# LSH attention with a routed MoE: the first head pair's projections, mask loads and factors in another order

## The chip, the cores and the metric

The kernel runs on one core of one Trainium2 chip. The metric is the device time of one execution in microseconds; three runs of the kernel before gave 714.1, 710.82 and 713.1, median 713.1. All times in the trace are in microseconds from the start of the profiled span.

## The reference

Attention with 4 batches, 8 heads, 768 tokens and 64 channels in which a query sees only the keys of its own hash bucket, then a mixture of 8 experts with one expert per token:

```python
q_bits = (np.einsum('bhsd,dk->bhsk', q, proj) > 0)      # 6 bits
k_bits = (np.einsum('bhsd,dk->bhsk', k, proj) > 0)
mask = q_bucket[:, :, :, None] == k_bucket[:, :, None, :]
scores = np.where(mask, scale * np.matmul(q, k.transpose(0, 1, 3, 2)), -1000000000.0)
attn = softmax(scores); out = np.matmul(attn, v)        # written out in the reference
x = out.transpose(0, 2, 1, 3).reshape(B * S, H * D)
expert_idx = argmax(x @ w_gate); y = relu(x @ w1[e]) @ w2[e]; return gate_w * y
```

## The kernel before

Two heads of one batch make a pair, and 16 pairs are worked one behind the other. A pair has 12 units: 128 queries of one head against all 768 keys. In the first pair units 0 to 2 and 3 to 5 are the two heads, in later ones the heads alternate; units 6 to 11 are the second half of the queries. Every instruction's place on its engine is written out by hand: a list of words for the first pair (`HEAD`, L956 to L960), one for each further pair (`PLAN`), one for the last (`LAST`), and `step` (L1025) turns a word into instructions. Each engine works its instructions in the order of the words.

What a word does (the digits behind it are the unit, or the head, and the part):

- S: the four matmuls of a unit's scores on TensorE, two with the low parts and the mask rows (L309), two with the high parts (L311). Three score tiles in PSUM; a fourth score waits for the exponential that read the first.
- R: the negated row maximum (`peak`, L319) on VectorE. In the first pair and the last pair R also makes the two factors that the exponential takes, scale and bias (`factor`, L324 and L326), on VectorE. In the pairs between, a word A makes them, on the engine that its letter names (P is GpSimd; there the second operation is L328).
- X: the exponential on ScalarE (L335), with the row sums.
- T and E: transposes of the exponentials on TensorE for units 0 to 5 (L349) and the copies out of PSUM, on ScalarE (E..a, L375) or VectorE (E..v, L373). D: 32x32 turns of units 6 to 11 on VectorE (L389); Y: SyncE then sends them between partitions, eight transfers a word (L400). B: products with the values (L411).
- G, H, w: the projections for the bucket bits of the next pair on TensorE (`lsh_mm`, L264; two PSUM tiles of the same two that T, B and K use), their signs on ScalarE (L244) and the store of the bits to memory (L277, L278; the store on SyncE).
- s and z: head 2 or 3 is split into parts of higher and lower precision on GpSimd (`split`, L192 to L199; head 2 is `w_214` in the order, head 3 `w_337`, their input `w_69`), and the bits are read back as mask rows of that head (`mask`, L282, issued by GpSimd). The word s04 makes the half of head 2's queries that unit 12, the first of pair 1, reads; s05 the other half. C words do the same for pairs from the third on.

On SyncE, loads of inputs and values and fills of rows in memory are issued ahead of a score by `before` (L1001), between the store of the bits and the exchange.

Of the kernel before, what the change touches and what calls it, by code (L numbers as in the profile page):

```python
# [15 lines left out]
B, H, S, D = 4, 8, 768, 64  # L16
# [3 lines left out]
NG = B * NP  # L20
# [36 lines left out]
def lsh_attention_moe(ctx, tc, qk2, v, proj, wg, w1, w1q, w2, out):  # L57
    nc = tc.nc
# [16 lines left out]
    def load_x(h):  # L75
        g = h // 2
        if g == NG - 1:
            x = (wk if h % 2 else moe).tile([128, 2 * S], F32, name="xl" if h % 2 else "xhe", bufs=1)
        else:
            x = room[:, h % 2] if g % 2 else wk.tile([128, 2 * S], F32, name="xd")  # L80
        for c in ((S, 2 * S), (0, S)) if h < 2 else ((0, 2 * S),):
            nc.sync.dma_start(x[:, c[0]:c[1]], qk2[h][:, c[0]:c[1]])
        XD[h] = x

    def load_v(g):
        VT[g] = wk.tile([128, NT, 2, D], F32, name="vt")
        nc.sync.dma_start(VT[g], v[g])
# [60 lines left out]
    def fill(e):  # L148

        nc.sync.dma_start(xs[e * ROW:e * ROW + FILL].rearrange("(p j) w -> p j w", p=128),  # L150
                          C["empty"][:, 0:1].to_broadcast([128, FILL // 128, RW]))
# [135 lines left out]
    def unit(i):  # L287

        g, r = divmod(i, 12)
        hf, r = divmod(r, 6)  # L290
        t, s = divmod(r, 2)
        if i < 6:
            s, t = divmod(r, 3)
        return g, hf, s, t

    def score(i, parts=None):
        parts = parts or ((False, True) if i < 4 else (True, False))
        g, hf, s, t = unit(i)
        k = QK[2 * g + s]
        if i not in SC:  # L300
            SC[i] = ps.tile([128, 2, 512], F32, name="s", bufs=3)
        p = SC[i]
        c = slice((3 * hf + t) * 128, (3 * hf + t) * 128 + 128)

        for low in parts:
            for a in range(2):
                n = slice(a * HALF, (a + 1) * HALF)
                if low:
                    nc.tensor.matmul(p[:, a, :HALF], k[0:80, 2, c], k[0:80, 3, n], start=i >= 4, stop=i < 4)  # L309
                else:  # L310
                    nc.tensor.matmul(p[:, a, :HALF], k[:, 0, c], k[:, 1, n], start=i < 4, stop=i >= 4)  # L311

    def peak(i):
        g, hf, s, t = unit(i)
        p = SC[i]
        if i % 6 == 0:
            SM[g, hf] = wk.tile([128, 3, 3], F32, name="sm", bufs=4)[:, :, 0:2]
        m = MB[i] = wk.tile([128, 4], F32, name="m", bufs=5)
        nc.vector.tensor_reduce(m[:, 0:1], p[:, :, :HALF], axis=AX.XY, op=OP.max, negate=True)  # L319

    def factor(i, eng):

        m = MB[i]
        eng.tensor_scalar(m[:, 1:2], m[:, 0:1], -FLOOR, D ** -0.5, op0=OP.is_lt, op1=OP.mult)  # L324
        if eng is nc.vector:
            eng.tensor_scalar(m[:, 2:3], m[:, 0:1], m[:, 1:2], None, op0=OP.mult)  # L326
        else:
            eng.tensor_tensor(m[:, 2:3], m[:, 0:1], m[:, 1:2], op=OP.mult)  # L328
# [54 lines left out]
    def turn(i):  # L383

        g, j = divmod(i, 12)
        if g not in DT:
            DT[g] = moe.tile([128, 4, 6, NT, 32], F32, name="w2")
        d = DT[g][:, :, j - 6]
        nc.vector.transpose(d.rearrange("p b k q -> p k b q"), PP.pop(i).rearrange("p a c -> p (a c)"))  # L389
# [14 lines left out]
    def pv(u, kt):  # L404
        g, hf = divmod(u, 2)
        if kt == 0:
            PV[u] = ps.tile([128, 512], F32, name="t", bufs=2)
        p = PV[u]
        for s in range(2):
            x = PT[u][:, :, s::2, kt].rearrange("p a t q -> p t a q") if turned(u) else PT[u][:, s, kt, :]  # L410
            nc.tensor.matmul(p[s * 64:(s + 1) * 64, :HALF], VT[g][:, kt, s, :], x,  # L411
                             start=(kt == 0), stop=(kt == NT - 1))

    def pv_end(u):
        OT[u] = wk.tile([128, HALF], F32, name="ot")
        nc.scalar.activation(OT[u], PV.pop(u)[:, :HALF], AF.Copy)
# [515 lines left out]
    def weight_half(op, x):  # L932
# [22 lines left out]

    HEAD = """  # L956
        k01A k00V j00V j01P y01 q00A p00V y00 q01P l00V b03 p01P f0 b00 b02 l01P b01 k10A f1 k11A y11 j10P p10A R0
        q10A S1 j11P b12 y10 R1 l10P b13 S2 X0 b10 p11P s01 R2 X1 b11 S3 q11P S4 X2 G H w R3 T00 T01 E00a l11P S5 R4
        E01a T02 X3 s00 R5 E02a s02 T10 X4 S6 E10v X5 R6 T11 S7 s10 E11a T12 s13 R7 E12a T20 X6 S8 s03 E20v T21 X7
        S9 z0 E21a T22 s11 R8 E22a D6 S10 s14 R9 X8 s15 D7 S11 R10 X9 s12 z1 B00 D8 R11 s05 X10 B01 s04 X11  # L960
    """.split()

    PLAN = """
# [37 lines left out]
    def before(c):  # L1001

        g, r = divmod(c, 6)
        if r == 3 and g + 2 < NG:
            load_x(2 * g + 4)
            load_x(2 * g + 5)
        if g + 1 < NG and r == (5 if g else 4):
            load_v(g + 1)
        for e in {(0, 1): (0,), (0, 2): (1,), (0, 3): (2,), (0, 4): (3,), (1, 4): (4,), (2, 4): (5,), (3, 4): (6,), (4, 4): (7,)}.get((g, r), ()):
            fill(e)  # L1010

    def behind(i):

        if i % 2 == 0:
            return
        c = i // 2
        if c == NC - 6:
            rows(0)
        if c >= NC - 6:
            weights((1, 1, 1, 2, 1, 2)[c - NC + 6])  # L1020
# [3 lines left out]
    def step(g, w):  # L1024

        prev = w.count("-")
        w = w.rstrip("-")
        n = g - prev
        if n < 0 or (g == NG and not prev):
            return  # L1030
        op, x = w[0], w[1:]
        if op == "S":
            i = 12 * n + int(x)
            if i % 2 == 0:
                before(i // 2)
            score(i)
        elif op == "R":
            i = 12 * n + int(x)
            peak(i)
            if not 0 < n < NG - 1:  # L1040
                factor(i, nc.vector)
                behind(i)
        elif op == "A":
            factor(12 * n + int(x[:-1]), ENG[x[-1]])
        elif op == "B":
            for kt in range(3 * int(x[1]), 3 * int(x[1]) + 3):
                pv(2 * n + int(x[0]), kt)
        elif op == "D":
            turn(12 * n + int(x))
        elif op == "Y":  # L1050
            exchange(n, ((0, 1), (2, 3))[int(x)])
        elif op == "C":
            part(2 * n + 2 + int(x[0]), int(x[1]))
        elif op == "Z":
            route_step(n, int(x))
        elif op == "N":
            scatter_step(n, int(x))
        elif op == "X":
            expo(12 * n + int(x))
        elif op == "T":  # L1060
            trans(6 * n + int(x[0]), int(x[1]))
        elif op == "E":
            trans_ev(6 * n + int(x[0]), int(x[1]), x[2] == "v" and not (n % NP == 1 and n > NP and x in FREE))
        elif op == "V":
            for kt in range(NT):
                pv(2 * n + int(x[0]), kt)
        elif op == "O":
            pv_end(2 * n + int(x))
        elif op == "M":
            sums(2 * n + int(x))  # L1070
        elif op == "K":
            TK[2 * n + int(x)] = tok(2 * n + int(x))
        elif op == "L":
            tok_ev(2 * n + int(x), TK.pop(2 * n + int(x)))
        elif op == "G" and n + 1 < NG:
            lsh_mm(n + 1)
        elif op == "H" and n + 1 < NG:
            lsh_ev(n + 1)
        elif op in "kjqlp":
            cut(op, int(x[0]), int(x[1]), x[2])  # L1080
        elif op == "y":
            lsh_first(int(x[0]), int(x[1]))
        elif op == "b":
            bits_first(int(x[0]), int(x[1]))
        elif op == "f":
            if x == "0":
                before(0)
            score(0, (x == "1",))
        elif op == "i":
            warmth(SC.setdefault(int(x[0]), ps.tile([128, 2, 512], F32, name="s", bufs=3))[:, 0], int(x[1]))  # L1090
        elif op == "s":
            split(2 + int(x[0]), int(x[1]))
        elif op == "z":
            mask(2 * n + 2 + int(x))
        elif op == "w":
            lsh_bits(n + 1)
        elif op in "xgh":
            xt_first(op, int(x))
        elif op == "m":
            mm1(0, int(x))  # L1100
        elif op in "ud":
            relu(op, int(x))
        elif op == "r":
            go(last[int(x)], 1)
        elif op == "c":
            scatter(B - 1, int(x))
        elif op in "nt":
            weight_half(op, x)
# [142 lines left out]
```

## Time and profile before

| what | value |
|---|---|
| median of three runs | 713.1 us |
| profiled execution | 714.13 us, span 712.0 us |
| TensorE busy | 693.6 us, 97% |
| VectorE, GpSimd, ScalarE busy | 495.0, 493.4, 405.9 us |
| first pair's first score to pair 1's first | 7.03 to 34.45 us |
| pair 1's first score to pair 2's | 34.45 to 60.97 us |

Busy shares are means over stages with different limits. A row of a timeline gives the start, the length, the engine, the line and what stands before it: in brackets the idle time of that engine and what ended it. Matmuls overlap, so the busy time of TensorE is not time at its peak. Where a wait is put down to an engine that had long been done, it was another, often a transfer.

### The profile page before, as it was taken

What the parts mean: (1) busy time and instruction counts of PE and PEld (TensorE: products, weight loads), DVE (VectorE), ACT (ScalarE), POOL (GpSimd) and SP (SyncE); (2) the same over time, 40 slices, a digit from 0 to 9 for tenths busy, and PEclk for the clock granted to TensorE, in tenths of its full rate; (3) what the DMA queues carried; (4) which work ended last, traced back from release to release, by engine and by line L of the source; (5) the groups of instructions that cost most, each with busy time, mean ns of one, the idle gap of its engine ahead of it and who ended that gap; (6) DMA issues with size and microseconds to landing.
All of it is one profiled execution on the core that took longest, in us unless ns stands there. A gap on an engine that the chain in (4) does not pass through costs nothing.

```text
span 712.0 us, 13593 instructions
## 1 busy us (share of the span) xinstructions
PE 693.6 (97%) x4539; PEld 558.8 (78%) x4539; DVE 495.0 (70%) x931; ACT 405.9 (57%) x813; POOL 493.4 (69%) x757
## 2 busy tenths in 40 slices
PE   8889999999999999999998999999999999999996
PEld 4677678667866776677566788899999999989895
DVE  7897898899888998898998672424766825232321
ACT  5876677668766876687576623544444444444310
POOL 8775776688778788976884664685666676768522
PEclk7999999999999999999999999999999999999998
DMA  9888899858866678787659338684847474747201
GB/s 329 273 204 254 260 260 240 248 177 237 258 192 209 204 199 250 216 241 208 193 172 254 93 141 213 209 219 121 200 133 187 140 196 138 207 150 201 94 12 39
DMA packets 67774, 138.32 MB, mean 194 GB/s; under 512 B 12883, under 2 KB 29523, under 8 KB 67680
## 3 DMA queue, kind: packets, MB, share of 16 engines
q1 hardware_dynamic: 60848, 120.67, 60.0%
q0 software_dynamic: 6688, 16.35, 6.8%
q8 instruction: 61, 1.00, 0.6%
q14 instruction: 33, 0.27, 0.1%
q10 hardware_dynamic: 144, 0.03, 0.0%
HBM read 75.79 MB, written 26.33 MB: 143 GB/s over the span
## 4 chain that ended last, share of the span: by engine, by line
PE 84%; DVE 6%; issue 4%; ACT 3%; POOL 1%; DMA 1%; SPq 0%; POOLq 0%; another core or an unknown queue 0%; DVEq 0%; ACTq 0%
PE s L769 28%; PE t L411 18%; PE s L309 9%; PE s L867 8%; PE s L311 8%; PE t L349 7%; DVE m L319 3%; PE t L430 3%; ACT e L335 2%; PE t L264 2%; PE s L876 1%; ACT pt L375 1%; DVE w L389 1%; POOL w L694 1%; DMA xd<-in_qk_dram 1%
## 5 line engine op out<-in xcount | busy, mean ns | idle before, releaser
L335 ACT ACTIVATE e<-s,m 128x768 f32<-128x768 f32 x192 | 189.7, 991 | 61.9 <-POOL m L328 39.3
L319 DVE TENSOR_REDUCE m<-s 128x1 f32<-128x768 f32 x192 | 179.8, 948 | 33.2 <-PE s L311 26.4
L694 POOL TENSOR_TENSOR w<-raw,w 128x512 fp32r<-128x512 f32 x112 | 145.0, 1320 | 35.3 <-ACT w L693 34.3
L411 PE MATMUL t<-pt,vt 128*64 128x384 f32 x768 | 130.9, 490 | 1.6 <-ACT e L335 1.5
L769 PE MATMUL s<-xh,w 128*128 128x432 f32 (+11 forms) x672 | 122.0, 338 | 0.1
L769 PEld LDWEIGHTS s<-xh,w 128*128 128x128 f32 x672 | 114.6, 188 | 3.2 <-issue 1.0
L411 PEld LDWEIGHTS t<-pt,vt 128*64 128x64 f32 x768 | 52.6, 137 | 65.8 <-issue 61.9
L829 DVE SCALAR_TENSOR_TENSOR hh<-s,hh 128x256 fp32r<-128x256 f32 (+7 forms) x64 | 35.5, 554 | 97.0 <-ACT hh L827 95.6
L349 PE MATMUL t<-ident,e 128*128 128x128 f32 x612 | 87.3, 276 | 4.2 <-DVE xr L440 2.1
L389 DVE STREAM_TRANSPOSE w<-e 128x768 f32<-128x768 f32 x90 | 82.7, 953 | 0.9 <-ACT e L335 0.4
L349 PEld LDWEIGHTS t<-ident,e 128*128 128x128 f32 x612 | 70.1, 141 | 15.0 <-ACT pt L375 3.4
L827 ACT ACTIVATE hh<-s 128x256 fp32r<-128x256 f32 (+7 forms) x64 | 31.3, 489 | 88.2 <-PE s L769 88.2
L769 PE MATMUL s<-hh,w 128*128 128x432 f32 (+5 forms) x384 | 72.4, 349 | 0.0
L693 ACT ACTIVATE w<-raw 128x512 fp32r<-128x512 f32 x112 | 66.7, 623 | 8.8 <-DMA raw<-in_w1q_dram 7.2
L769 PEld LDWEIGHTS s<-hh,w 128*128 128x128 f32 x384 | 70.0, 188 | 1.3
L880 POOL DMA_INDIRECT out_dram<-y,ix x26 | 26.9, 1033 | 57.1 <-DVE y L878 23.2
L324 POOL TENSOR_SCALAR m<-m 128x1 f32<-128x1 f32 x112 | 25.6, 229 | 58.6 <-DVE m L319 57.4
L309 PE MATMUL s<-w 80*128 80x384 f32 x192 | 57.1, 378 | 2.9 <-ACT e L335 2.6
L309 PE MATMUL s<-qk 80*128 80x384 f32 x192 | 57.6, 383 | 1.1 <-ACT e L335 1.0
L867 PE MATMUL s<-w,hh 128*128 128x512 f32 (+1 forms) x240 | 56.4, 394 | 0.0
L375 ACT ACTIVATE pt<-t 128x512 f32<-128x512 f32 (+1 forms) x96 | 53.4, 586 | 4.2 <-PE t L349 2.3
L867 PEld LDWEIGHTS s<-w,hh 128*128 128x128 f32 (+1 forms) x240 | 44.6, 187 | 10.5
(222 smaller groups left out, 1073.4 us busy)
## 6 DMA issues: line engine op xcount, KB each, us to landing
pt<-w SPq DMA_DIRECT2D x240, 144.0 KB, 3.2
raw<-in_w_dram SPq DMA_DIRECT2D x36, 512.0 KB, 3.8
raw<-in_w1q_dram SPq DMA_DIRECT2D x28, 512.0 KB, 4.7
w<-in_qk_dram SPq DMA_DIRECT2D x14, 768.0 KB, 6.5
xd<-in_qk_dram SPq DMA_DIRECT2D x14, 768.0 KB, 7.2
sorted_rows<-xr SPq DMA_DIRECT2D x8, 1156.0 KB, 11.1
vt<-in_v_dram SPq DMA_DIRECT2D x16, 384.0 KB, 3.7
xg<-sorted_rows SPq DMA_DIRECT2D x16, 256.0 KB, 7.1
```

What stands on the lines that cost most here:

```text
L309: nc.tensor.matmul(p[:, a, :HALF], k[0:80, 2, c], k[0:80, 3, n], start=i >= 4, stop=i < 4)
L311: nc.tensor.matmul(p[:, a, :HALF], k[:, 0, c], k[:, 1, n], start=i < 4, stop=i >= 4)
L319: nc.vector.tensor_reduce(m[:, 0:1], p[:, :, :HALF], axis=AX.XY, op=OP.max, negate=True)
L335: nc.scalar.activation(e, p[:, :, :HALF], AF.Exp, bias=m[:, 2:3], scale=m[:, 1:2], accum_out=SM[g, hf][:, t, s:s + 1])
L349: nc.tensor.transpose(p[:, x * 128:(x + 1) * 128], e[w][:, kt // 3, (kt % 3) * 128:(kt % 3) * 128 + 128], ident)
L375: nc.scalar.activation(o, x, AF.Copy)
L389: nc.vector.transpose(d.rearrange("p b k q -> p k b q"), PP.pop(i).rearrange("p a c -> p (a c)"))
L411: nc.tensor.matmul(p[s * 64:(s + 1) * 64, :HALF], VT[g][:, kt, s, :], x, start=(kt == 0), stop=(kt == NT - 1))
L693: nc.scalar.activation(w[:, 0, a], r, AF.Copy)
L694: nc.gpsimd.tensor_tensor(w[:, 1, a], r, w[:, 0, a], op=OP.subtract)
L769: nc.tensor.matmul(p[:, :z], w, x[:, :z], start=first and k == 0, stop=k == len(ts) - 1 and (n < 2 or not first))
L867: nc.tensor.matmul(p[:pw], HH[n][b][:, f, i:i + pw], w[:, a, f % 4], start=(k == 0), stop=(k == 23))
```

## The change

Only the first pair's words and what goes with them change. The projections for pair 1 (G) move from ahead of the first transposes to behind the score of unit 6; their signs and the store move accordingly. The factors of units 6 to 11 of the first pair go to GpSimd (A6P to A11P), placed between the splits. The mask loads z0 and z1 move behind more of the splits. The input loads for pair 2 and two row fills are issued one or two units later.

```diff
     HEAD = """
...
-        q10A S1 j11P b12 y10 R1 l10P b13 S2 X0 b10 p11P s01 R2 X1 b11 S3 q11P S4 X2 G H w R3 T00 T01 E00a l11P S5 R4
+        q10A S1 j11P b12 y10 R1 l10P b13 S2 X0 b10 p11P s01 R2 X1 b11 S3 q11P S4 X2 R3 T00 T01 E00a l11P X3 S5 R4
...
     def before(c):
 
         g, r = divmod(c, 6)
-        if r == 3 and g + 2 < NG:
+        if r == (3 if g else 4) and g + 2 < NG:
             load_x(2 * g + 4)
             load_x(2 * g + 5)
...
-        for e in {(0, 1): (0,), (0, 2): (1,), (0, 3): (2,), (0, 4): (3,), (1, 4): (4,), (2, 4): (5,), (3, 4): (6,), (4, 4): (7,)}.get((g, r), ()):
+        for e in {(0, 1): (0,), (0, 2): (1,), (0, 4): (2,), (0, 5): (3,), (1, 4): (4,), (2, 4): (5,), (3, 4): (6,), (4, 4): (7,)}.get((g, r), ()):
             fill(e)
...
             peak(i)
+            if n == NG - 1 or i < 6:
+                factor(i, nc.vector)
             if not 0 < n < NG - 1:
-                factor(i, nc.vector)
                 behind(i)
```

TensorE in the first pair, from the second half of unit 4's scores on, before: L264 are the 32 projections (16 rows of two instructions), L349 the transposes, L309 and L311 scores.

```order
L311 MATMUL s<-qk 128x384 x2
L264 MATMUL t<-w_69,pj 32x192 x16
L349 MATMUL t<-ident,e 128x128 x8
L309 MATMUL s<-qk 128x384 x2
L311 MATMUL s<-qk 128x384 x2
L349 MATMUL t<-ident,e 128x128 x8
```

The same place now:

```order
L311 MATMUL s<-qk 128x384 x2
L349 MATMUL t<-ident,e 128x128 x8
L309 MATMUL s<-qk 128x384 x2
L311 MATMUL s<-qk 128x384 x2
L349 MATMUL t<-ident,e 128x128 x4
L309 MATMUL s<-qk 128x384 x2
L311 MATMUL s<-qk 128x384 x2
L264 MATMUL t<-w_69,pj 32x192 x16
L309 MATMUL s<-qk 128x384 x2
L311 MATMUL s<-qk 128x384 x2
L349 MATMUL t<-ident,e 128x128 x8
```

The projections stand behind two more scores and three of the nine transpose steps, between the scores of units 6 and 7.

VectorE at units 5 to 8 before, from the peak of unit 5: L319 is a peak, L324 and L326 its factors, L373 a copy of transposed tiles.

```order
L319 TENSOR_REDUCE m<-s 128x1
L324 TENSOR_SCALAR m<-m 128x1
L326 TENSOR_SCALAR m<-m 128x1
L373 COPY pt<-t 128x2x128 x2
L319 TENSOR_REDUCE m<-s 128x1
L324 TENSOR_SCALAR m<-m 128x1
L326 TENSOR_SCALAR m<-m 128x1
L319 TENSOR_REDUCE m<-s 128x1
```

The same place now, again from the peak of unit 5:

```order
L319 TENSOR_REDUCE m<-s 128x1
L324 TENSOR_SCALAR m<-m 128x1
L326 TENSOR_SCALAR m<-m 128x1
L319 TENSOR_REDUCE m<-s 128x1
L373 COPY pt<-t 128x2x128 x2
L319 TENSOR_REDUCE m<-s 128x1 x2
L373 COPY pt<-t 128x2x256
```

The factors from unit 6 on are gone, and the two copies stand between the peaks of units 6 and 7 instead of ahead of both.

GpSimd from the first split of head 2 on, before: L192 to L199 are splits, L282 a mask load.

```order
L192 CAST w_214<-w_69 128x768
L196 TENSOR_TENSOR w_214<-w_69,w_214 80x384
L192 CAST w_337<-w_69 128x768
L196 TENSOR_TENSOR w_337<-w_69,w_337 80x384
L196 TENSOR_TENSOR w_214<-w_69,w_214 80x384
L282 DMA w_214<-masks 16x4x384
L194 CAST w_337<-w_69 128x768
```

The same place now (head 3 is `w_351` here); L324 and L328 are the factors of a unit, from unit 6 on.

```order
L192 CAST w_214<-w_69 128x768
L196 TENSOR_TENSOR w_214<-w_69,w_214 80x384
L324 TENSOR_SCALAR m<-m 128x1
L328 TENSOR_TENSOR m<-m 128x1
L196 TENSOR_TENSOR w_214<-w_69,w_214 80x384
L324 TENSOR_SCALAR m<-m 128x1
L328 TENSOR_TENSOR m<-m 128x1
L192 CAST w_351<-w_69 128x768
L324 TENSOR_SCALAR m<-m 128x1
L328 TENSOR_TENSOR m<-m 128x1
L194 CAST w_351<-w_69 128x768
```

The factors of units 6, 7 and 8 stand behind the second, third and fourth split. Those of unit 9 follow two splits later; then come two splits, the first mask load, unit 10, one half of head 3's query low part, unit 11, the second mask load, and last the two halves of head 2 (s05, s04), as before.

## Rows read from the trace of the kernel before

**Rows 1.** The page, part 4: the chain that ended last, shares of the span by engine.
```profile
PE 84%; DVE 6%; issue 4%; ACT 3%; POOL 1%; DMA 1%; SPq 0%; POOLq 0%; another core or an unknown queue 0%; DVEq 0%; ACTq 0%
```

**Rows 2.** The chain of waits, 0 to 80 us: start, us, what.
```profile
34.21 2.60 DVE w L389 x3
...
38.44 0.82 ACT e L335
```

**Rows 3.** Timeline, TensorE: start us, us, engine line operation shapes count, idle before.
```profile
16.85 1.53 PE L264 MATMUL t<-w,pj 64*32 64x192 f32 x32
18.95 1.09 PE L349 MATMUL t<-ident,e 128*128 128x128 f32 x8 [0.57 <-ACT bits L244]
...
30.43 4.09 PE L411 MATMUL t<-pt,vt 128*64 128x384 f32 x24
...
34.91 0.51 PE L311 MATMUL s<-w 128*128 128x384 f32 x2
...
39.58 0.62 PE L309 MATMUL s<-w 80*128 80x384 f32 x2 [1.24 <-ACT e L335]
...
41.13 0.60 PE L349 MATMUL t<-ident,e 128*128 128x128 f32 x4
...
52.03 2.16 PE L411 MATMUL t<-pt,vt 128*64 128x384 f32 x12 [1.50 <-ACT e L335]
```

**Rows 4.** Timeline, VectorE, 22 to 25 us.
```profile
22.32 0.75 DVE L373 COPY pt<-t 128x256 f32<-128x256 f32 x2
23.09 0.96 DVE L319 TENSOR_REDUCE m<-s 128x1 f32<-128x768 f32 x1
...
24.42 0.96 DVE L319 TENSOR_REDUCE m<-s 128x1 f32<-128x768 f32 x1
```

**Rows 5.** Timeline, ScalarE: one exponential.
```profile
20.71 0.98 ACT L335 ACTIVATE e<-s,m 128x768 f32<-128x768 f32 x1
```

**Rows 6.** Timeline, GpSimd, 17 to 52 us.
```profile
17.22 1.95 POOL L196 TENSOR_TENSOR w<-w,w 80x384 fp32r<-80x384 f32 x2
...
24.27 0.84 POOL L194 CAST w<-w 128x768 fp32r<-128x768 f32 x1
25.04 0.51 POOL L198 CAST w<-w 64x384 fp32r<-64x384 f32 x1
...
26.67 0.50 POOL L198 CAST w<-w 64x384 fp32r<-64x384 f32 x1
...
29.61 0.54 POOL L282 DMA_DIRECT2D w<-masks  x1 [0.31 <-POOL w L196]
...
33.38 0.82 POOL L208 CAST qk<-xd 128x768 fp32r<-128x768 f32 x1
...
35.71 1.98 POOL L214 TENSOR_TENSOR qk<-xd,qk 80x384 fp32r<-80x384 f32 x2
...
51.17 0.23 POOL L324 TENSOR_SCALAR m<-m 128x1 f32<-128x1 f32 x1
...
51.64 0.99 POOL L216 TENSOR_TENSOR qk<-xd,qk 64x384 fp32r<-64x384 f32 x1
```

**Rows 7.** Timeline, SyncE: the second half of the first exchange.
```profile
43.45 4.96 SPq L400 DMA_DIRECT2D pt<-w  x8
```

**Rows 8.** DMA issues of 23 to 25 us: queue, KB, us to landing.
```profile
w<-masks POOLq DMA_DIRECT2D x1, 96.0 KB, 7.9
```

**Rows 9.** DMA issues of 29 to 31 us.
```profile
w<-masks POOLq DMA_DIRECT2D x1, 96.0 KB, 5.8
```

**Rows 10.** Stretches: us, busy us (count) of PE, PEld, DVE, ACT, POOL, granted clock, DMA.
```profile
8.50:15.00 6.50, 6.50 (x19) 3.61 (x16) 3.87 (x8) 3.99 (x8) 6.21 (x8) 0.50 1.05 390
...
50.00:53.00 3.00, 1.50 (x10) 0.78 (x10) 2.93 (x5) 2.54 (x5) 2.92 (x6) 1.00 0.98 300
705.00:708.00 3.00, 0.85 (x8) 0.62 (x6) 0.48 (x1) 0.00 (x0) 0.97 (x1) 1.00 0.09 26
708.30:712.00 3.70, 0.00 (x0) 0.00 (x0) 0.00 (x0) 0.00 (x0) 0.00 (x0) 0.50 0.05 14
```

More of the change, by code (lines that the diff above doesn't have):

```diff
@@ L957, in lsh_attention_moe @@
         k01A k00V j00V j01P y01 q00A p00V y00 q01P l00V b03 p01P f0 b00 b02 l01P b01 k10A f1 k11A y11 j10P p10A R0
-        q10A S1 j11P b12 y10 R1 l10P b13 S2 X0 b10 p11P s01 R2 X1 b11 S3 q11P S4 X2 G H w R3 T00 T01 E00a l11P S5 R4
-        E01a T02 X3 s00 R5 E02a s02 T10 X4 S6 E10v X5 R6 T11 S7 s10 E11a T12 s13 R7 E12a T20 X6 S8 s03 E20v T21 X7
-        S9 z0 E21a T22 s11 R8 E22a D6 S10 s14 R9 X8 s15 D7 S11 R10 X9 s12 z1 B00 D8 R11 s05 X10 B01 s04 X11
+        q10A S1 j11P b12 y10 R1 l10P b13 S2 X0 b10 p11P s01 R2 X1 b11 S3 q11P S4 X2 R3 T00 T01 E00a l11P X3 S5 R4
+        E01a T02 s00 X4 R5 E02a s02 S6 G R6 A6P S7 H X5 s03 w T10 E10v R7 A7P T11 S8 X6 s10 E11a T12 R8 A8P E12a s11
+        T20 X7 S9 E20v s13 R9 A9P T21 X8 E21a s12 T22 E22a D6 s14 z0 S10 R10 A10P X9 D7 s15 S11 R11 A11P z1 X10 D8
+        B00 s05 X11 B01 s04
     """.split()
```

## The prediction

> **What bounds the kernel now.** I read four views, in this order. The page's chain first: it lies on TensorE for 84% of the span and on VectorE for 6% [rows 1]; so a change far from TensorE counts only where TensorE then waits. Next the chain of waits through the first two head pairs, because the edits lie in the first. There the chain leaves TensorE at about 20 us and goes down VectorE, peak, scale, bias, turn, until the last three turns end at 36.81 and an exponential follows at 38.44 [rows 2]. So the first pair is VectorE's, and what is gained or lost there shows where TensorE takes over again. TensorE's timeline gives those places: the last products of pair 0 from 30.43 to 34.52, the second half of the first score of pair 1 at 34.91, a wait of 1.24 before 39.58 and a wait of 1.50 before 52.03 [rows 3]. The first wait is an exponential behind VectorE's late turns. For the second the row names ScalarE, but what the products at 52.03 read is the turned tile that SyncE sends through eight transfers until 48.41 [rows 7], which then have to land. Those two waits, 2.74 us, are all the slack that pair 1 has. Last I read GpSimd's timeline, because the change gives it work. Its last split of heads 2 and 3 ends when the first cast for pair 2 begins, at 33.38 [rows 6], 1.5 us ahead of the score that reads it. That margin is the number to watch.
>
> **What the change takes off VectorE.** Peaks 6 and 7 start at 23.09 and 24.42 [rows 4]: 1.33 apart, of which the peak itself is 0.96, so scale and bias cost 0.37. Six of them leave: 2.2 us of the chain of pair 0, if nothing else is late.
>
> **What the moved projections do.** The 32 projections took 1.53 us at 16.85, and the transposes behind them came at 18.95 after 0.57 more of waiting for the bits [rows 3]. The transposes now start at 16.85, 2.10 sooner. TensorE still runs at the lower of its levels there (granted 0.50 from 8.5 on [rows 10]), and transposes that took 1.09 may take twice that, so 1.0 to 2.1 us of it reach unit 6: its peak comes at 21.0 to 22.1 instead of 23.09. Unit 7 does not gain this. The projections now stand between units 6 and 7 on TensorE, and the pair of copies of 0.75 that VectorE did before peak 6 [rows 4] now stands between peaks 6 and 7. The same work precedes peak 7 in both kernels, less one scale and bias. I keep its old start, 24.42, with 1 us either way.
>
> **What GpSimd gets, and in which order.** This is the term that decides. An engine takes its instructions in order, and the factors of units 6 to 11 are put between the splits. The factor of unit 6 stands behind only the first two splits of head 2 and waits for peak 6; the factor of unit 7 stands one split further and waits for peak 7. Before, it had by 25.04 [rows 6] also done two casts and a subtraction of head 3 and issued the first mask load. Now it idles until peak 7 ends at 24.42 + 0.96 = 25.4, and its factor, 0.47 from 51.17 to the next instruction at 51.64 [rows 6], ends at 25.9. From here nothing on GpSimd waits any more; each peak is done before its factor's turn. What is left of the first pair's list, with steps between starts in [rows 6]: two casts of a whole head at 0.77 (24.27 to 25.04), 1.54; two subtractions at half of 1.95, 1.95; four halves of the query low part (cast and subtraction) at 1.63 (25.04 to 26.67), 6.52; four factors at 0.47, 1.88; two mask loads at 0.54, 1.08. Sum 12.97, so the last split of head 2 ends at 38.9 instead of 33.38. It is the half that the first score of pair 1 reads. Bounds: 37.9 to 39.9 by peak 7.
>
> **What TensorE then waits for.** The second half of the first score starts at 38.95 instead of 34.91: 4.0 us late, all of it idle after products that end at about 34.5 as before. Behind it are 0.51 for that half, the next projections with at most 1.53 [rows 3] and then the first score of head 3, so by 41.0. That score reads the second mask load, which stands ahead of the two halves of head 2: it is issued at 38.9 - 3.26 - 0.54 = 35.1. The two loads of before took 7.9 and 5.8 us to land [rows 8, 9], so it lands at 40.9 or 43.0. I take 5.8, the row of the same load of head 3: the transfers ahead of it start some 5 us later now, and so does the load. The first mask load stands 3.1 us before it (its own 0.54, two factors, one half), at 32.0, and lands at 37.8 to 39.9, about when the split ends.
>
> The lateness runs on through GpSimd. Behind the last split stand five parts of head 5, from 33.38 to 37.69 before [rows 6], 4.31 us, and behind those the factor of the second unit of pair 1, which the exponential of that unit reads, which the first transposes of pair 1 read. That is 38.9 + 4.31 + 0.47 = 43.7, one exponential of 0.98 with its read of the sum, 1.1 [rows 5], so the transposes start at 44.85 instead of 41.13: 3.7 us late. From there TensorE worked without a wait for 9.40 us, until 50.53, and then waited 1.50 for the exchange [rows 3]. Now it comes to that place at 54.25. VectorE's last turn moves little (its exponential needs the last factor, now done at 35.1, so the turn ends near 37 as before); the exchange is at most 1 us later and no longer waited for. Loss: 54.25 - 52.03 = 2.2 us. The gain on VectorE, 2.2, is thus not to be had: the wait for GpSimd replaces it.
>
> **The clock.** A pause of over 4 us is new in this kernel. The rows have a pause on either side of it: 1.50 us between 50 and 53 left the clock at 1.00; at the end TensorE has no work after 705.85, and from 708.3 the clock is 0.50 [rows 10]. I expect it to fall to 1.2 GHz. What it costs depends on how long it stays down. From 8.5 to 15.0 it stayed at 0.50 with TensorE busy throughout [rows 10]. Bounds: nothing, and 5 us of lost work for 10 us at half speed. I take 1.1, near the lower end, because GpSimd, not TensorE, sets the 44.85 above, so slow matmuls before it are mostly hidden.
>
> **Sum.** 2.2 + 1.1 = 3.3 us later, and pair 2 and all after it follow TensorE without slack, so this stays. The profiled execution took 714.13 for a span of 712.0, so 717.4 in that execution; the median of the runs shown, 713.1, is 1.0 lower, so 716.4.
>
> **What else the change moves.** The store of the bits and the input loads behind it on SyncE go from 20 to about 25 us. The loads for pair 2 took until the first cast at 33.38 at most; 5 us later is still ahead of 38.9. Price nothing; if GpSimd were on time, up to 1 us.
>
> **Rivals.**
> 1. The masks too: the second load lands after 7.9 us, at 43.0 instead of 40.9, and the clock stays down for a second stretch. For: the fills ahead of it are now later and it may meet them undrained. Against: 5.8 was seen at the same place of GpSimd's list. Price 2.1 and 1.7 less what overlaps: in all 5.5 us slower, 718.6.
> 2. The clock does not fall, or falls where TensorE waits anyway: 2.2, 715.3.
> 3. GpSimd keeps up. It does if the last split ends by 34.4, that is if peak 7 ends before 21; then VectorE's 2.2 us are kept and the pair's waits of 1.24 shrink: 2.5 us faster, 710.6. Against: peak 7 cannot precede the projections.
> 4. The moved projections keep the clock low for longer. They were the last of TensorE's work before it rose; transposes stand there now. If it stays at half for 3 to 7 us more, peaks 6 and 7 and so GpSimd's list move by 0.6 to 2.3: some 4.8 in all, 717.9. The Trainium skill (TensorE: Matmul & The Clock Gate, Part 4: PE-mode transpose) says that transposes do not count as busy in the way that matmuls do. No run here shows transposes at the lower level; before, they come after the rise.
> 5. Nothing is left of it: slack elsewhere takes it up: 713.1. Against: after pair 1 the chain stays on TensorE for tens of us.
>
> **How the numbers follow.** Forecast 45% (half a microsecond to either side of 3.5 decides its class); rival 1 20%; rival 2 17%; rival 3 6%; rival 4 7%; rival 5 5%. About 0.5%, or 3.6 us, is what a measurement tells from no change. Slower by more: 20 of the forecast's 45, rivals 1 and 4 nearly whole: 46%. Faster by more: half of rival 3: 3%. Within: 51%. The range takes in rival 3's edge and rival 1 with a microsecond of spread from run to run: 712.3 to 720.3; the forecast's own is 714.5 to 718.5.
>
> **What would show it.** In the changed profile: GpSimd idle for 5 us before its first factor and 2 before its second; then no idle until about 38.9, where head 2's last split ends; TensorE idle for about 4 us before 39, released by GpSimd; the clock at 0.50 for some us behind that; no wait before the exchanged products, now near 54; from there a constant shift. It is wrong if TensorE goes from pair 0 to pair 1 at about 34 without a wait, or if the shift at the second pair's exchange is under 1 us.

## The result and the profile after

| | before | after |
|---|---|---|
| median of six runs | 712.28 us (710.28 to 714.1) | 718.77 us (717.54 to 721.0) |
| profiled execution | 714.13 us, span 712.0 | 717.54 us, span 715.4 |
| second half of pair 1's first score | 34.91 | 38.14 |
| second half of pair 2's first score | 61.43 | 63.29 |

The change makes the kernel slower by 6.5 us, ratio 1.0092 with interval 1.0071 to 1.0114. The forecast was 716.4, with 714.5 to 718.5 around it and 712.3 to 720.3 for the whole range: the median lies 2.4 above the forecast. The two profiled executions lie only 3.4 us apart: that of before is the longest of its six runs and that of after the shortest of its six. This matters below.

The page's chain after (shares of the span by engine) answers to [rows 1]:

```profile
PE 85%; issue 4%; ACT 3%; DVE 2%; POOL 2%; DMA 1%; POOLq 0%; another core or an unknown queue 0%; DVEq 0%; ACTq 0%
```

VectorE's share falls from 6% to 2%, GpSimd's rises from 1% to 2%. The first pair has changed its owner, and TensorE's timeline after shows what that does (start, length, engine, line and operation, in brackets the idle time before and what ended it):

```profile
14.15 1.03 PE L349 MATMUL t<-ident,e 128*128 128x128 f32 x8
...
17.28 0.52 PE L311 MATMUL s<-qk 128*128 128x384 f32 x2
...
18.77 0.88 PE L264 MATMUL t<-w,pj 64*32 64x192 f32 x30 [0.53 <-ACT pt L375]
...
24.44 1.00 PE L349 MATMUL t<-ident,e 128*128 128x128 f32 x4 [1.55 <-ACT pt L375]
...
30.30 4.09 PE L411 MATMUL t<-pt,vt 128*64 128x384 f32 x24
37.72 0.59 PE L309 MATMUL s<-w 80*128 80x384 f32 x2 [3.33 <-DMA w<-masks]
38.14 0.75 PE L311 MATMUL s<-w 128*128 128x384 f32 x2
38.82 1.53 PE L264 MATMUL t<-xd,pj 64*32 64x192 f32 x32
40.29 1.01 PE L309 MATMUL s<-w 80*128 80x384 f32 x2
...
44.78 0.44 PE L349 MATMUL t<-ident,e 128*128 128x128 f32 x2 [0.56 <-ACT e L335]
...
53.89 2.16 PE L411 MATMUL t<-pt,vt 128*64 128x384 f32 x12
...
62.84 0.62 PE L309 MATMUL s<-qk 80*128 80x384 f32 x2
```

The last products of pair 0 start at 30.30, as before at 30.43 [rows 3]. Behind them is a pause of 3.33 us that was not there. The score at 40.29, which reads the second mask load, has no wait. The exchanged products at 53.89 have no wait any more, where [rows 3] show 1.50.

GpSimd's timeline after, first pair, answers to [rows 6]; L324 opens a factor, L282 is a mask load, L196 to L199 are splits, L208 is the first cast for pair 2:

```profile
19.21 0.26 POOL L324 TENSOR_SCALAR m<-m 128x1 f32<-128x1 f32 x1 [2.69 <-DVE m L319]
...
22.73 0.22 POOL L324 TENSOR_SCALAR m<-m 128x1 f32<-128x1 f32 x1 [2.02 <-DVE m L319]
...
27.87 0.22 POOL L324 TENSOR_SCALAR m<-m 128x1 f32<-128x1 f32 x1 [1.67 <-DVE m L319]
...
30.82 0.77 POOL L282 DMA_DIRECT2D w<-masks  x1
...
34.23 0.61 POOL L282 DMA_DIRECT2D w<-masks  x1
...
37.00 0.99 POOL L199 TENSOR_TENSOR w<-w,w 64x384 fp32r<-64x384 f32 x1
38.06 0.82 POOL L208 CAST qk<-xd 128x768 fp32r<-128x768 f32 x1
```

Three factors stand at the head of the queue and wait for their peaks, 6.4 us in all. The splits and both mask loads stand behind them, so the cast that closes the list comes at 38.06 instead of 33.38 [rows 6]. Not all of these 4.7 us is waiting. GpSimd was idle in the first pair of before too, for the bits that its first mask load reads:

```profile
23.52 0.74 POOL L282 DMA_DIRECT2D w<-masks  x1 [4.36 <-DMA masks<-bits]
```

With the 0.31 of [rows 6] that is 4.67 us, so idle time grew by only 1.7. The six factors themselves, at about 0.47 each, are another 2.8. What the idle time stands ahead of has changed as well: two splits stand ahead of the first wait now, where five stood before, and eight instead of five ahead of the first mask load. Ahead of the second there are nine in both kernels. In the chain of waits (start, length, what) the first mask load ends the pause:

```profile
30.82 6.76 DMA w<-masks
37.58 0.14 issue
37.72 0.59 PE s L309 x2
```

The last split ends at 37.99, 0.4 us behind the mask, and the second half of the score starts at 38.14: masks and splits are late together.

Stretches after (from and to; busy time of PE, PEld, DVE, ACT and POOL with counts; granted clock; DMA share; GB/s) answer to [rows 10]:

```profile
8.50:15.00 6.50, 5.97 (x34) 3.83 (x33) 5.88 (x13) 5.31 (x11) 6.13 (x9) 1.00 1.05 388
...
34.50:37.70 3.20, 0.00 (x0) 0.02 (x1) 1.21 (x3) 1.28 (x3) 3.04 (x5) 1.00 0.89 293
38.40:41.60 3.20, 3.20 (x38) 1.99 (x37) 1.33 (x3) 1.15 (x3) 3.20 (x5) 0.50 0.97 232
...
359.20:362.40 3.20, 3.04 (x12) 2.95 (x13) 2.11 (x4) 1.52 (x3) 1.77 (x4) 0.50 0.92 258
```

From 8.50 to 15.00 the clock stood at its upper level (2.4 GHz), where before it stood at 0.50 [rows 10]. So the two profiles do not differ by the change alone. After the pause it is at the lower level for some microseconds, as forecast; a third such stretch, at 359, is taken up at the end.

### The profile page after: what moved, and what is told of

Same layout as the page of the kernel before. It is cut to its first block, busy times and chain, and to the rows that moved or that the text cites. A ratio compares the mean times of both kernels' runs of the same rounds, so it can differ in the third digit from the quotient of the medians.

```text
span 715.4 us, 13601 instructions
## 1 busy us (share of the span) xinstructions
PE 693.7 (97%) x4539; PEld 560.0 (78%) x4539; DVE 493.1 (69%) x919; ACT 405.4 (57%) x813; POOL 495.7 (69%) x769
## 4 chain that ended last, share of the span: by engine, by line
PE 85%; issue 4%; ACT 3%; DVE 2%; POOL 2%; DMA 1%; POOLq 0%; another core or an unknown queue 0%; DVEq 0%; ACTq 0%
PE s L769 28%; PE t L411 17%; PE s L309 10%; PE t L349 8%; PE s L311 8%; PE s L867 8%; PE t L430 3%; PE t L264 2%; ACT e L335 2%; DVE m L319 1%; PE s L876 1%; DMA w<-masks 1%; ACT pt L375 1%; POOL w L694 1%; DVE xr L440 0%
## 5 line engine op out<-in xcount | busy, mean ns | idle before, releaser
L319 DVE TENSOR_REDUCE m<-s 128x1 f32<-128x768 f32 x192 | 179.9, 950 | 33.3 <-PE s L311 30.3
L349 PE MATMUL t<-ident,e 128*128 128x128 f32 x612 | 89.2, 280 | 5.5 <-ACT pt L375 2.4
L349 PEld LDWEIGHTS t<-ident,e 128*128 128x128 f32 x612 | 72.1, 143 | 15.8 <-ACT pt L375 5.0
L324 POOL TENSOR_SCALAR m<-m 128x1 f32<-128x1 f32 x118 | 27.0, 229 | 66.4 <-DVE m L319 64.2
L309 PE MATMUL s<-w 80*128 80x384 f32 x192 | 57.3, 380 | 5.0 <-DMA w<-masks 3.3
L309 PE MATMUL s<-qk 80*128 80x384 f32 x192 | 57.5, 381 | 1.1 <-ACT e L335 0.9
```

The costliest lines, as they stand in the source:

```text
L349: nc.tensor.transpose(p[:, x * 128:(x + 1) * 128], e[w][:, kt // 3, (kt % 3) * 128:(kt % 3) * 128 + 128], ident)
```

## The experiments

Theory: GpSimd works in order, so factors that wait for peaks delay the splits and mask loads behind them, pair 1 starts late, and the pause also lowers the clock. Rivals: the moved projections cost time by themselves; the factors cost time by themselves; the clock alone does it. In the table "pair 1" and "pair 2" are the second half of their first score in the trace, in us. The three groups, e1 to e4, e5 to e8 and e9 to e12, each on a chip of its own, had their own runs of the kernel before, medians 712.81, 713.82 and 713.07.

| kernel | median | ratio to before, interval | pair 1 | pair 2 |
|---|---|---|---|---|
| e1, factors on VectorE | 713.82 | 1.0018, 1.0006 to 1.003 | 34.65 | 60.03 |
| e2, factors alone | 716.09 | 1.004, 1.0022 to 1.0058 | 39.03 | 63.45 |
| e3, filled pause | 717.75 | 1.0079, 1.0059 to 1.0098 | 38.52 | 62.53 |
| e4, splits first | 716.97 | 1.0058, 1.0037 to 1.0078 | 36.11 | 64.36 |
| e5, before, clock held | 711.51 | 0.9967, 0.9949 to 0.9984 | 32.90 | 58.35 |
| e6, after, clock held | 716.65 | 1.0044, 1.0021 to 1.0066 | 38.01 | 61.93 |
| e7, splits and masks first | 714.03 | 1.0001, 0.9978 to 1.0025 | 34.91 | 60.84 |
| e8, e1 with clock held | 712.59 | 0.9978, 0.9956 to 1.0 | 33.21 | 59.67 |
| e9, e5 with masks earlier | 712.35 | 0.9985, 0.9965 to 1.0005 | 31.67 | 58.40 |
| e10, e7 with clock held | 712.62 | 1.0004, 0.9978 to 1.003 | 33.18 | 58.32 |
| e11, e8 with a copy earlier | 713.35 | 0.9998, 0.9973 to 1.0023 | 34.16 | 64.63 |
| e12, e5 again | 712.00 | 0.9992, 0.9967 to 1.0016 | 32.91 | 57.76 |

### The two halves of the change (e1, e2)

e1 is the changed kernel with the factors of the first pair left on VectorE:

```diff
-E01a T02 s00 X4 R5 E02a s02 S6 G R6 A6P S7 H X5 s03 w T10 E10v R7 A7P T11 S8 ...
+E01a T02 s00 X4 R5 E02a s02 S6 G R6 S7 H X5 s03 w T10 E10v R7 T11 S8 ...
...
-            if n == NG - 1 or i < 6:
+            if n == NG - 1 or n == 0:
                 factor(i, nc.vector)
```

> The changed kernel, but the factors of units 6 to 11 of the first pair are made by VectorE again, right behind each peak; the later projections, the later mask loads and the later input loads stay. Theory (factors on GpSimd hold up the splits behind them): GpSimd no longer waits for peaks, its last split of head 2 ends before 35, no pause of TensorE over 1.5 us before pair 1, time 711 to 713.5, as before. Rival (the late bits and mask loads do the harm): the first score of pair 1 still waits for its mask rows until 36 or later, 715 or more. Rival (the clock does it, by the moved projections): 715 or more with a clock that is lower through the first pair and no pause.

Measured: 713.82, within 0.2% of before and 0.3 us above the range of the theory. GpSimd's first mask load and TensorE's first score of pair 1 in e1:

```profile
24.13 0.74 POOL L282 DMA_DIRECT2D w<-masks  x1 [1.68 <-DMA masks<-bits]
```

```profile
30.17 4.09 PE L411 MATMUL t<-pt,vt 128*64 128x384 f32 x24
34.19 0.62 PE L309 MATMUL s<-w 80*128 80x384 f32 x2
```

No pause behind the products, and the mask is asked for at 24.13 instead of 30.82. By the ratios 0.18% of the 0.92% is left, so some four fifths of the loss hang on the factors' engine. The rest is clear of 1 (1.0006 to 1.003): with the factors on VectorE, the other parts of the change cost about 1 us.

e2 is the kernel before with A6P to A11P put right behind their peaks and nothing else:

```diff
-E01a T02 X3 s00 R5 E02a s02 T10 X4 S6 E10v X5 R6 T11 S7 s10 E11a T12 s13 R7 E12a ...
+E01a T02 X3 s00 R5 E02a s02 T10 X4 S6 E10v X5 R6 A6P T11 S7 s10 E11a T12 s13 R7 A7P E12a ...
```

> The kernel before, with one thing of the change: the factors of units 6 to 11 go to GpSimd, each at the place of its peak in the old order. Projections, mask loads and input loads stay where they were. Theory (factors): GpSimd waits for peaks 6 and 7 as in the changed kernel, head 2's last split ends near 39, TensorE pauses 4 us before pair 1, 715 to 719. Rival (late bits and masks): within 1 us of before, 711 to 713.5.

Measured: 1.004. GpSimd in e2:

```profile
23.00 0.26 POOL L324 TENSOR_SCALAR m<-m 128x1 f32<-128x1 f32 x1 [6.37 <-DVE m L319]
...
37.98 0.99 POOL L199 TENSOR_TENSOR w<-w,w 64x384 fp32r<-64x384 f32 x1
```

The stall at the factor is there without the moved projections, and the last split ends at 38.97. The expected pause of 4 us before pair 1 is not there. TensorE loses its time earlier, at a score of pair 0 that waits for a late exponential, and at half clock behind that (0.53 from 30 to 34, 0.50 from 34 to 37), where the products take 6.58 instead of 4.09:

```profile
30.43 1.01 PE L309 MATMUL s<-qk 80*128 80x384 f32 x2 [2.44 <-ACT e L335]
...
32.01 6.58 PE L411 MATMUL t<-pt,vt 128*64 128x384 f32 x24
```

So the time is in the range of the theory, but here the factors that come late behind the splits do the harm as well as the splits behind the factors. The two halves add up to 0.58% where the whole change costs 0.92% (1.0071 to 1.0114): roughly a third of it comes only with both, though intervals this wide fix that share poorly.

### The clock in the pause (e3)

e3 is the changed kernel with 14 matmuls of ones ahead of pair 1, into a score tile that is then overwritten:

```diff
+        if g == 1:
+            SC[12] = ps.tile([128, 2, 512], F32, name="s", bufs=3)
+            warmth(SC[12][:, 0], 14)
```

> The changed kernel with 14 full matmuls of ones (3.0 us at full clock) put into TensorE's pause before the first score of pair 1, into the score tile that this score then overwrites. Rival (much of the loss is the clock that falls in the pause): the granted clock stays at 1.00 from 36 to 45, and the time is 2 to 3 us below the changed kernel, 716 to 717. Theory (the wait itself is the loss, the clock a small part): at most 1 us below it, 717.5 to 719.

Measured: 717.75, ratio 1.0079. TensorE in e3, and the stretch behind the pause:

```profile
34.30 3.19 PE L106 MATMUL s<-ones 128*128 128x512 bf16 x14
38.09 0.59 PE L309 MATMUL s<-w 80*128 80x384 f32 x2 [0.59 <-POOL w L199]
```

```profile
38.20:41.60 3.40, 3.25 (x44) 2.35 (x44) 2.07 (x4) 1.66 (x4) 3.40 (x5) 1.00 0.95 229
```

The clock does not fall and pair 2 comes 0.76 us sooner than after (62.53 against 63.29); by the ratios it is 0.9 us, though their intervals overlap. In these two executions the gain does not reach the end: both spans are 715.4. The clock in the pause is a small part of the loss, as the theory had it.

### GpSimd's order (e4, e7)

e4 puts all splits of head 2 early and the first mask load ahead of unit 9's factor; e7 also puts the second mask load and head 3's split there. The words that differ in e7:

```diff
-E01a T02 s00 X4 R5 E02a s02 S6 G R6 A6P S7 H X5 s03 w T10 E10v R7 A7P T11 S8 X6 s10 E11a T12 R8 A8P E12a s11
-T20 X7 S9 E20v s13 R9 A9P T21 X8 E21a s12 T22 E22a D6 s14 z0 S10 R10 A10P X9 D7 s15 S11 R11 A11P z1 X10 D8
-B00 s05 X11 B01 s04
+E01a T02 s00 X4 R5 E02a s02 S6 G R6 s03 s04 A6P S7 H X5 s05 w T10 E10v R7 A7P T11 S8 X6 s10 E11a T12 R8 A8P z0 E12a s11
+T20 X7 S9 E20v s13 R9 s12 z1 A9P T21 X8 E21a T22 E22a D6 S10 R10 A10P X9 D7 s14 S11 R11 A11P X10 D8
+B00 s15 X11 B01
```

In e4 the second of these lines is `T20 X7 S9 E20v s13 R9 A9P T21 X8 E21a s12 T22 E22a D6 s14 S10 R10 A10P X9 D7 z1 S11 R11 A11P X10 D8`, the others are as in e7.

> The changed kernel, all its factors on GpSimd and its projections late, but GpSimd's own list in another order: all five splits of head 2 stand first, two more of them ahead of the first factor and one ahead of the second, then head 3's; the first mask load behind factor 8, the second behind factor 10, head 3's last half last. Theory (what hurts is that splits stand behind factors that wait): GpSimd idles under 1.5 us before its first factor, head 2 is whole by 23, the pause before pair 1 shrinks to under 1.5 us, 712 to 714.5. If the loss came from the factors' own length or from the way over GpSimd: 717 or more.

> The splits-first kernel (all factors on GpSimd, head 2's splits first) with head 3's mask load two splits and two factors earlier, right behind the three splits that write what the mask rows overwrite. If the mask load of head 3 is what still holds up pair 1 there (TensorE waited 2.63 us for it): that wait falls under 1 us, and the time to 713 to 715.5. If the rest of the splits-first loss is something else: 716 to 718.

TensorE in e4:

```profile
35.68 0.59 PE L309 MATMUL s<-w 80*128 80x384 f32 x2 [0.16 <-DMA w<-masks]
...
40.06 0.98 PE L309 MATMUL s<-w 80*128 80x384 f32 x2 [2.63 <-DMA w<-masks]
```

With the splits out of the way the pause shrinks to 0.16, and comes back one score later as a wait for the second mask load: 1.0058, 716.97 where 712 to 714.5 was expected. So mending the splits alone is not enough. TensorE in e7:

```profile
34.91 0.51 PE L311 MATMUL s<-w 128*128 128x384 f32 x2
...
37.27 0.59 PE L309 MATMUL s<-w 80*128 80x384 f32 x2 [0.96 <-DMA w<-masks]
```

e7 has every instruction of the changed kernel, the moved projections and the factors on GpSimd, and only GpSimd's order differs. It is level with before, 1.0001 (0.9978 to 1.0025), and both its wait and its median are where they were expected. So the order on GpSimd carries the whole loss, within 1.8 us.

### The same with the clock held (e5, e6, e8, e10, e12)

Three matmuls of ones (the word i03) stand directly ahead of the first score, at the place that some expectations call ahead of the first heads' transposes. In all seven traces with this word (e5, e6, e8 to e12) the clock is at 1.00 from 8.50 to 34. Without it, it is at 1.00 from 8.50 to 15.00 in three traces (after, e1, e3) and lower in four (before 0.50, e2 0.60, e4 0.50, e7 0.59). They too write a score tile that is then overwritten.

```diff
-k01A k00V j00V j01P y01 q00A p00V y00 q01P l00V b03 p01P f0 ...
+k01A k00V j00V j01P y01 q00A p00V y00 q01P l00V b03 p01P i03 f0 ...
```

e5 and e12 are before with this word, e6 after with it and with 12 matmuls in the pause, e8 is e1 with it, e10 is e7 with it.

> The kernel before with three full matmuls of ones in TensorE's wait before its first score (0.64 us at full clock in a wait of 0.80), so that the clock has less cause to fall in the first pair. In the runs of before the time rises with the lost clock (1 minus the mean granted clock, times the span) by about 0.4 us per us. If the clock in the first pair is what moves before from run to run: granted clock 0.997 or more in most runs and 710 to 711.5. If the pause before the first score has no part in it: clock and time as before, 712 to 713.5.

> The changed kernel with the same three matmuls before the first score and 12 in the pause before pair 1. Its distance to the kernel before with the three matmuls is the loss at a clock that is held in both. If waiting for GpSimd and the masks is about 3.5 of the 6.5 us and the clock 3: clock 0.993 or more, 714.5 to 716, 3 to 4.5 above e5. If the clock is no part of it: 717.5 to 719.

> The changed kernel with its factors on VectorE and the three matmuls before the first score. It is the later projections, masks and input loads alone at a held clock, against e5. If these alone cost about 1 us, as e1 against before: 711 to 712.5, 1 above e5. If e1's 1 us was clock: within 0.5 of e5.

> e7 (the change with the splits and both mask loads ahead of the factors on GpSimd) with three matmuls of ones ahead of the first heads' transposes, so that the clock is held. If the six factors cost time only by delaying splits and mask loads, this stands level with e8 (the moved projections, no factors on GpSimd, held clock): first score of pair 2 at 59.3 to 60.2 us, median within 0.8 us of e8's 712.6. Rival (the factors cost in themselves, by VectorE's normalisation or GpSimd's own chain waiting for them): first score of pair 2 at 61 us or later, and median about 2 to 4 us above e8's, near e6's 716.7.

> The kernel of e5 (the kernel before with three matmuls of ones ahead of the first heads' transposes) on the same chip as e9 to e11, since their differences are about a microsecond and chips differ by as much. If the held clock is worth what e5 showed: 0.2 to 0.5 per cent below the kernel before, and the first score of pair 2 at 58.2 to 58.6 us with no half clock in the first pair. If e5 was an accident of that chip: level with the kernel before, within 0.1 per cent.

TensorE in e5, then in e6, then in e10: the first scores of pair 1 and the exchanged products.

```profile
32.90 0.61 PE L311 MATMUL s<-w 128*128 128x384 f32 x2 [0.84 <-POOL w L199]
...
48.95 2.16 PE L411 MATMUL t<-pt,vt 128*64 128x384 f32 x12 [0.89 <-ACT pt L375]
```

```profile
37.58 0.59 PE L309 MATMUL s<-w 80*128 80x384 f32 x2 [2.15 <-DMA w<-masks]
...
52.53 2.16 PE L411 MATMUL t<-pt,vt 128*64 128x384 f32 x12
```

```profile
36.01 0.59 PE L309 MATMUL s<-w 80*128 80x384 f32 x2 [1.44 <-DMA w<-masks]
...
48.93 2.16 PE L411 MATMUL t<-pt,vt 128*64 128x384 f32 x12
```

With the clock out of the comparison the change still costs 3.6 us at pair 2 (61.93 against 58.35) and 5.1 in the medians (716.65 against 711.51), more than the 3 to 4.5 that was expected. e10 takes that back: its exchanged products start at 48.93, as in e5, pair 2 comes at 58.32, and its median is 0.6 above e12's with overlapping intervals. So the moved projections and the factors on GpSimd together cost nothing measurable once GpSimd's order is right, and together they gain nothing.

e5 came out at 711.51 as expected, with a granted clock of 0.997 or more in nine of its twelve executions. e8 lies 1.1 above it, as expected too. At pair 2 it is 1.3 us behind e5, which I read as the price of the moved projections. TensorE's waits in e8:

```profile
24.54 0.66 PE L349 MATMUL t<-ident,e 128*128 128x128 f32 x4 [1.50 <-ACT pt L375]
...
50.27 2.16 PE L411 MATMUL t<-pt,vt 128*64 128x384 f32 x12 [1.35 <-ACT e L335]
```

e10 has the projections in the same place and is not behind. That does not settle the price of the projections: in e8 the chain runs from 26.0 to 36.7 through VectorE's peaks, factors and turns, and e10 has six pairs of factors less there, so their move may pay what the projections cost. No run has the moved projections with the mask loads of e10 and the factors on VectorE. Against e8's 59.67, e10's 58.32 at pair 2 is 1.35 sooner, earlier than the 59.3 to 60.2 expected; the medians are level (712.62 and 712.59, on two chips). The row names an exponential for the wait at 50.27, but e8's last exchange transfers, issued at 46.2, took 3.8 us to land, until 50.0; the products wait for those.

e12 repeats e5 on another chip: pair 2 at 57.76 and no half clock in the first pair, but a median only 1.1 us below before, and by the ratio 0.08%, with an interval that holds 1: level within the 0.1% that was to show e5's gain as an accident of its chip. By the two medians a held clock is worth 1.1 to 2.3 us to the kernel before; only e5's is clear of noise.

### What else was tried (e9, e11)

e9 changes e5's order on GpSimd so that the second mask load comes earlier:

```diff
-S9 z0 E21a T22 s11 R8 E22a D6 S10 s14 R9 X8 s15 D7 S11 R10 X9 s12 z1 B00 D8 R11 s05 X10 B01 s04 X11
+S9 z0 E21a T22 s11 R8 E22a D6 S10 s12 z1 R9 X8 s14 D7 S11 R10 X9 s04 B00 D8 R11 s05 X10 B01 s15 X11
```

> The kernel before, with three matmuls of ones ahead of the first heads' transposes (as in e5) and GpSimd's work of the first pair in another order: the splits for pair 1 as s11, s12, second mask load, s14, s04, s05, s15, where e5 has s11, s14, s15, s12, second mask load, s05, s04. GpSimd order theory (what stands ahead of pair 1's first scores on GpSimd sets when they start): in e5 the first score waited 0.84 us for the last split of head 2 and the next unit 0.45 us for its mask, so both waits go and the first score of pair 2 comes up to 1.3 us earlier than e5's 58.35 us; median 710.3 to 711.5 against e5's 711.5. Rival (pair 1 is set by something else by then, VectorE's sums or the exponentials): the waits only move to later units, first score of pair 2 stays within 0.4 us of 58.35 and the median within 0.5 us of e5's. Against the kernel before: 0.3 to 0.5 per cent faster by either.

TensorE in e9:

```profile
36.33 0.62 PE L309 MATMUL s<-w 80*128 80x384 f32 x2 [1.24 <-ACT e L335]
...
49.00 2.16 PE L411 MATMUL t<-pt,vt 128*64 128x384 f32 x12 [0.83 <-ACT pt L375]
```

Pair 1's first score comes 1.2 us sooner than in e5, and pair 2 not at all (58.40 against 58.35): the rival was right, the waits move. With the clock held, GpSimd alone is not what bounds pair 1 in the kernel before.

e11 is e8 with one copy of ScalarE ahead of an exponential:

```diff
-... S6 G R6 S7 H X5 s03 w T10 E10v R7 T11 S8 X6 s10 E11a T12 R8 E12a s11
+... S6 G R6 S7 H X5 s03 w T10 E10v R7 T11 S8 E11a X6 s10 T12 R8 E12a s11
```

> e8 (the moved projections, factors on VectorE, held clock) with one copy on ScalarE, the evacuation of head 1's transposed tile, put ahead of the exponential of unit 6 instead of behind it. Theory: the moved projections cost 1.1 to 1.3 us because they and the transposes behind them end on copies that stand behind exponentials on ScalarE (e8's 1.50 us wait at 24.5 us): with the copy earlier that wait shrinks by about an exponential's 0.6 to 0.9 us, the first score of pair 2 comes 0.5 to 1.2 us earlier than e8's 59.67, and the median lies at 711.5 to 712.2. Rival (the exponential pushed back costs as much, or the cost of the move lies in the later waits, 1.81 us at 38.0 and 1.35 us at 50.3): first score of pair 2 within 0.3 us of 59.67 and the median level with e8's 712.6.

Measured: 713.35, no gain, and neither of the two places expected for pair 2; the wait at 24.5 is gone, but pair 2 comes 5.0 us later than in e8. GpSimd and TensorE in e11:

```profile
46.46 0.58 POOL L282 DMA_DIRECT2D qk<-masks  x1 [0.68 <-DMA masks<-bits]
...
50.72 0.23 POOL L324 TENSOR_SCALAR m<-m 128x1 f32<-128x1 f32 x1
```

```profile
52.57 4.11 PE L411 MATMUL t<-pt,vt 128*64 128x384 f32 x12 [3.13 <-ACT e L335]
```

This is the same mechanism at another place: the mask load waits at the head of GpSimd's queue for bits that landed at 46.18, a factor stands behind it, an exponential behind the factor, and TensorE waits 3.13 us. The clock is at 0.50 behind that, from 52 to 58. The profiled execution is the longest of this kernel's twelve (716.99 against a median of 713.35), so it shows how the loss arises and not its usual size.

No version beats the kernel before for certain: e5 does on one chip; the intervals of e8, e9 and e12 reach 1. e7 and e10 beat the changed kernel.

## Why the prediction came out as it did

- **GpSimd decides: right.** Idle before the first factor 2.69 (forecast 5), before the second 2.02 (2), the last split late, TensorE idle for 3.33 (4.0), the exchanged products unwaited at 53.89 (54.25). The shift behind is constant, 1.86 at pair 2 and 1.85 at 357.54, until the clock falls at 359; at the end it is 3.4. e7 shows that the order is the cause, by changing nothing else.
- **When the peaks come: wrong, and made up for.** The second factor started at 22.73, not 25.4, since the clock was up from 8.50 to 15.00; in e4, whose clock was at 0.50 there as in before, it starts at 25.55. "From here nothing on GpSimd waits any more" was wrong too: unit 9's factor waits 1.67 more, behind transposes that waited 1.55 for ScalarE. The two errors cancel in the main, by luck, so the split ends at 37.99 against 38.9. The work between, without that wait, took 37.99 - 23.18 - 1.67 = 13.1, against a sum of 12.97.
- **Masks: right in kind, undervalued.** The first load took 6.76 and landed at 37.58, inside the forecast's 37.8 to 39.9 but for 0.2. I let the split end the pause and the mask come "about when the split ends"; the mask comes first by 0.4, and e4 shows that mending the splits alone gives back only a part. Rival 1 forecast 718.6, next to the measured 718.77, but by a wait for the second load, and the score that reads it, at 40.29, has none: that nearness is luck.
- **The clock behind the pause: right, 1.1 forecast, about 0.8 to 0.9 measured** (e3). Rival 2, that it stays up, failed. Rival 4 has nothing for it: in e4, whose clock was at 0.50 in 8.50 to 15.00 with transposes where before has the projections, it rose in the same microsecond as in before, between 18 and 19 (its eight transposes at 16.84 take 1.90 us, against 1.03 at 14.15 after). The Trainium skill (TensorE: Matmul & The Clock Gate, Part 4: PE-mode transpose) says that transposes do not count as busy as matmuls do. After, the granted clock is still 1.00 in a stretch that has eight transposes at 14.15, but scores stand between them, so no run here shows transposes alone.
- **The term that was mis-sized: "Loss: 54.25 - 52.03 = 2.2".** The two profiled executions give 53.89 - 52.03 = 1.86 and differ by 3.4 at the end, near the forecast's 3.3, but they are not alike: the 52.03 belongs to an execution of before whose first pair ran 10 us at half clock, and after's 53.89 to one without that. With the clock held in both, before comes to that place at 48.95 (e5; 48.36 in e12) and after at 52.53 (e6). So the term is 3.6 in those traces and 5.1 in the medians. I corrected that execution only by the 1.0 us to the median, as if it differed from the others by that alone.
- **The clock in the other executions: not in the sum.** The six of after have a median granted clock of 0.986, against 0.992 to 0.994 in the three groups of before, and their times go from 717.54 at 0.992 to 721.0 at 0.983, by a straight line through the six about 0.5 us for each us of lost clock (1 minus the clock, times the span). By an estimate from these numbers, after's 10.0 us of lost clock against before's 4.3 to 5.7 makes 2 to 3 us of the 6.5. With the 3.6 that is 6 or so. Where these executions lose it cannot be seen, for the only profile of after is its fastest execution. Both kernels gain from a higher clock: held, before's median is 1.1 to 2.3 lower (e5, e12) and after's 2.1 (e6 against the result above, not side by side, and with the pause filled as well).
- **Projections at no loss: open.** Together with the factors on GpSimd in the right order they cost nothing measurable (e10 against e12). With the factors on VectorE, e1 is about 1 us behind before and e8 1.1 behind e5, the latter with overlapping intervals.
- **The 2.2 us on VectorE that cannot be had: right, but the reason given is not all of it.** The prediction puts the wait for GpSimd in its place. In e10 GpSimd waits for its first two factors 0.30 and 1.46 instead of 2.69 and 2.02 and its order is mended, and still nothing is gained: TensorE waits 1.44 there for the second mask load. So rival 3, 2.5 us faster once GpSimd keeps up, has no support either.
- **Open:** why the held-clock loss is 3.6 at pair 2 and 2.6 between the two profiled spans, but 5.1 in the medians. e5's profiled execution is the second longest of its twelve (it loses some clock at 354), e6's the second shortest of its twelve (it loses none there); where the executions without a profile lose theirs cannot be seen.

## What to carry to other kernels

A short instruction moved to an idle engine brings its wait along: before moving it, list what stands behind it in that queue and who waits for that, transfers included, and put those first. Read the granted clock in the stretch that carries the sum before using a place in one execution as the base, and when it is at the lower level, look for that place at the higher one in both kernels. A stretch that is bound by several engines gives little for any one of them: e9 removed two waits of pair 1 and the end did not move.

## What the runs showed of the hardware that was not expected

The same wait lowers the clock in one execution and not in another. Half way through, TensorE sat idle 1.66 us before 355.69 in the profiled execution of before, with the clock at 1.00 behind it. The same place after, in TensorE's timeline:

```profile
357.54 0.66 PE L349 MATMUL t<-ident,e 128*128 128x128 f32 x4 [1.69 <-DVE xr L440]
```

Here the clock was at 0.50 from 359.20 to 362.40, as the stretch above shows, and in e5, with 1.71 us of idle at the same place, it fell as well. The length of the wait does not sort them: after 1.70 in e6 it stayed at 1.00, after 1.32 in e3 it fell. And three matmuls ahead of the first score go with ten microseconds of clock in the kernel before: 0.50 from 8.50 to 15.00 in [rows 10], 1.00 in e5 and e12. As the clock is at 1.00 there in some traces without them too (after, e1, e3), it is the seven traces of seven that speak for them, and not the one pair.
